# Where a burst schedule runs its transposed maxima and sums: behind a stretch of projection steps, or inside it

## The chip, the core and the metric

The kernel runs on one core of a Trainium2 chip. The metric is the device time of one execution in microseconds (us); less is better. The engines run side by side, each in its own program order, and wait for one another through semaphores: TensorE (PE; PEld is its loading of weights), VectorE (DVE), ScalarE (ACT), GpSimd (POOL) and SyncE (SP), which here only issues transfers (DMAs). SPq is SP's queue of them. Matmuls write into PSUM, whose banks are handed out by tags of a pool: a tile of a tag with three buffers can be written only when the reader of the tile three before it is done.

## What is computed

Two kinds of layer alternate, twice: windowed attention and a filter in the frequency domain. The input is 2048 tokens by 576 features, with 32 heads of 18 features.

```python
def _A_ref(x, wqkv, wo):
    H = 32; Dh = D // H; W = 256
    qkv = (x @ wqkv).reshape(B, S, 3, H, Dh).transpose(2, 0, 3, 1, 4)
    q, k, v = qkv[0], qkv[1], qkv[2]
    scores = jnp.einsum("bhqd,bhkd->bhqk", q, k) * (Dh ** -0.5)
    mask = (idx[:, None] - idx[None, :] >= 0) & (idx[:, None] - idx[None, :] < W)
    p = softmax(jnp.where(mask, scores, -1e9), axis=-1)
    o = jnp.einsum("bhqk,bhkd->bhqd", p, v)
    return o.transpose(0, 2, 1, 3).reshape(B, S, D) @ wo

def _B_ref(x, w_r, w_i):
    X = jnp.fft.rfft2(x, axes=(-2, -1)) * (w_r + 1j * w_i)
    return jnp.fft.irfft2(X, s=(S, D), axes=(-2, -1))

for layer in (_A_ref, _B_ref, _A_ref, _B_ref):
    x = x + layer(layernorm(x))
```

The change lies in the attention layer (`layer_a`), which runs twice.

## The kernel before

**Tiles.** The 32 heads go in eight groups (n) of four (two `pair` by two `hp`), the 2048 tokens in 16 tiles (i or j) of 128, and these in four columns (c) of 512. A number x stands for (n, i): x = 16 n + i, from 0 to 127.

**Projections.** Queries and keys come from `proj(i, c)`, which is 14 steps (L801), each one matmul of 512 columns into one PSUM tile `pj`. After the 14th, ACT copies the high part to `sg`, and DVE later subtracts it to get the low part (the "remainder", L816), which SP stores to DRAM with it (`qk_d<-sg`, L818). `stack_load(n, c)` brings rows of several heads back from there into `qs` and `ks`: twelve transfers on SP (L833).

**Scores and maxima.** `score_max(x, pair, hp)` makes one tile of scores on PE (S, L857), and DVE takes its row maxima under the mask into a column of `m` (L859: the reduction, and a reading of its accumulator). When the four tiles of a column c are done for all four heads, `m_rows(n, c)` brings the maxima into the queries: PE transposes `m` into a PSUM tile of tag S (`tpm`, L865), ACT negates it into `mt` (L867), and four transfers on SP put its rows into row 63 of `qs` (L872). From then on a product of `ks` and `qs` has the maximum already taken off.

**Exponentials, sums, norms.** `exps(x, pair, hp)` makes such a product (E, L889), ACT takes the exponential into `P` (L890), and POOL zeroes what the window leaves out (L892, L895). `part(x, half)` multiplies `P` with the values, which carry a column of ones so that the sums of the rows come with it, into the one PSUM tile U (L909). After four tiles ACT copies U into `us`, a single buffer (L914), and `norm(n, c)` finishes the column: four transpositions on PE into a tile of tag S (`tpo`, L923), the reciprocal of the sums (`rc`, L926) and the product (`o`, L928) on DVE, and a transfer to DRAM on SP (L933).

**The bursts.** Most of the layer's work runs in `bursts()` (L968 to L1011), 136 bursts numbered by k. Each takes three E (e) and three S (c), the latter ten x ahead (`LEAD`); on PE in the order S, E, E, E, S, S, so that DVE has the first of a burst's maxima before the others. Behind them come the remainders that are due, the parts of U that `gaps` gives to this burst, and, in every odd k, a stretch of projection steps: five, five and four in turn, so that three stretches are one projection of 14 steps (near the end: four, four, three, three). `loads(x)` calls `stack_load` at the start of the burst in which an x that is divisible by four begins, and its transfers enter SP's queue there. A group of maxima is complete, and is appended to the list `due`, in the burst whose scores reach the end of a column; a norm is appended after the part that fills U. Both come every 16 thirds of a burst. E needs a column's maxima two tiles ahead of its own, so that, between the last score of a column and the first E that uses its maxima, there are 16 E (in the first column of a head group there are 24). The list is worked off only behind a stretch:

```python
if k % 2:
    m = left.pop(0)
    for f in pj[at:at + m]:
        f()
    ends, at = at // 14 != (at + m) // 14, at + m
    for f, *a in due[:len(due) - 1 if ends else 2]:
        f(*a)
        due.pop(0)
```

`ends` is true where the stretch closes a projection; all but one of the list are then run, which with one item is none. Nothing is reordered by a scheduler: each engine runs its instructions in the order in which this program issues them.

Of the kernel before, what the change touches and what calls it, by code (L numbers as in the profile page):

```python
# [608 lines left out]
def layer_a(tc, ident, eps, bp, src, dst, wqk_d, wv_d, wo_d, dc_d, gc_d, dram, copy, wvs, second, spectral, share):  # L609
# [17 lines left out]
    if True:  # L627
# [134 lines left out]
        with ExitStack() as c2:  # L762
# [20 lines left out]
            def remainders():  # L783
                while ended:
                    ended.pop(0)()
# [60 lines left out]
            def score_max(x, pair, hp):  # L846

                n, i = divmod(x, NT)
                c, t = divmod(i, 4)
                q, k = qs[n % 2], ks_[n % 2]  # L850
                if (n, c) not in ms:
                    ms[n, c] = wp.tile([128, 2, 2, 4], F32, tag="m", name=f"m{n}_{c}", bufs=3)
                lo, hi = max(0, i - 2) * 128, (i + 1) * 128
                N = hi - lo
                b = 64 * hp
                ps = pp.tile([128, 512], F32, tag="S", name=f"S{x}_{pair}_{hp}", bufs=3)
                T.matmul(ps[:, 0:N], q[b:b + 63, pair, i * 128:i * 128 + 128], k[b:b + 63, pair, lo:hi], start=True, stop=True)  # L857
                jk = wp.tile([128, 384], BF, tag="jk", name=f"jk{x}_{pair}_{hp}", bufs=3)
                V.tensor_tensor_reduce(out=jk[:, 0:N], in0=ps[:, 0:N], in1=mask[:, 384 - N:384], scale=1.0, scalar=-3e38,  # L859
                                       op0=ALU.add, op1=ALU.max, accum_out=ms[n, c][:, hp, pair, t:t + 1])  # L860
# [16 lines left out]
            def exps(x, pair, hp):  # L877

                n, j = divmod(x, NT)
                q, k = qs[n % 2], ks_[n % 2]  # L880
                nq = min(3, NT - j) * 128
                hl_ = 2 * hp + pair
                if hp == pair == 0:
                    pt[n, j] = wp.tile([128, 4, 384], F32, tag="P", name=f"P{n}_{j}", bufs=6)
                p = pt[n, j]

                ps = pp.tile([128, 512], F32, name=f"E{x}_{hl_}", **(dict(tag="S", bufs=3) if pair and NX - LEAD <= x < NX - 4 else dict(tag="E", bufs=3)))
                b = 64 * hp
                T.matmul(ps[:, 0:nq], k[b:b + 64, pair, j * 128:j * 128 + 128], q[b:b + 64, pair, j * 128:j * 128 + nq], start=True, stop=True)  # L889
                A.activation(p[:, hl_, 0:nq], ps[:, 0:nq], AF.Exp, scale=SC)  # L890
                if hp == pair == 1:
                    P.affine_select(out=p[:, :, 0:128], in_=p[:, :, 0:128], pattern=[[0, 4], [1, 128]], compare_op=ALU.is_ge,  # L892
                                    fill=0.0, base=0, channel_multiplier=-1)
                    if nq == 384:
                        P.affine_select(out=p[:, :, 256:384], in_=p[:, :, 256:384], pattern=[[0, 4], [-1, 128]], compare_op=ALU.is_gt,  # L895
                                        fill=0.0, base=0, channel_multiplier=1)
# [3 lines left out]
            def part(x, half):  # L900
                n, i = divmod(x, NT)

                e = i - i % 2
                j = (i - 1, i - 2 + 2 * (i % 2))[half]
                q0 = e if j < i else i
                q1 = e + 2 if i - 1 == j else q0 + 1
                for h in range(4):
                    if j >= 0:
                        T.matmul(U[32 * h:32 * h + 19, (q0 % 4) * 128:(q0 % 4) * 128 + 128 * (q1 - q0)], vts[n][:, j, h],  # L909
                                 pt[n, j][:, h, (q0 - j) * 128:(q1 - j) * 128],  # L910
                                 start=j == max(e - 1, 0), stop=j == i or (i == e and j == i - 2), skip_group_check=True)
                if half and i % 4 == 3:
                    us[n, i // 4] = u = wp.tile([128, 512], F32, tag="us", name=f"us{n}_{i}", bufs=1)
                    A.copy(u, U)  # L914
# [32 lines left out]
            pj = [f for i in range(2, 9) for c in range(4) for f in proj(i, c, c % 2 if i == 2 else c == 0 and i == 3)]  # L947
            done, due = 0, []
# [4 lines left out]
            def loads(t):  # L953
                n, c = divmod(t + 20, NT)
                if c % 4 == 0 and 0 < n < NQ:
                    stack_load(n, c // 4)
                if t + LEAD == 5:
                    v_load(0)
                if t + 12 in range(NT, NX, NT):
                    v_load((t + 12) // NT)  # L960

            def copies(t):
                if copy and t >= 32 and t % 4 == 0 and t < 32 + 16 * len(copy):

                    z, r = divmod(t // 4 - 8, 4)
                    P.dma_start(*[a[32 * r:32 * r + 32] for a in copy[z]])

            def bursts():  # L968

                es = [(x, pair, hp) for x in range(2, MIX) for pair in range(2) for hp in range(2)]  # L970
                ss = [(x + LEAD, pair, 1 - hp) for x, pair, hp in es]
                left = [*(5, 5, 4) * 20, *(4, 4, 3, 3) * 2]
                gaps = {}
                for p in range(2 * MIX - 5):
                    g = 2 * ((p + 1) // 3)
                    if p % 8 == 0 and p and (p + 1) % 3:
                        g += (p + 1) % 3
                    elif p % 8 == 1 and p > 1 and (p + 1) % 3 == 2:
                        g += 1
                    gaps.setdefault(g, []).append(divmod(p, 2))  # L980
                at = done
                for k in range(len(es) // 3):
                    e, c = es[3 * k:3 * k + 3], ss[3 * k:3 * k + 3]
                    for x, pair, hp in e:
                        if pair == hp == 0:
                            loads(x)
                            copies(x)
                    score_max(*c[0])
                    for f in e:
                        exps(*f)  # L990
                    score_max(*c[2])
                    score_max(*c[1])
                    remainders()
                    for x, half in gaps.get(k, ()):
                        part(x, half)
                        if half and x % 4 == 3:
                            due.append((norm, *divmod(x // 4, 4)))
                    full = (3 * k + 3) // 4 + 11
                    if (3 * k) // 4 + 11 < full and full % 4 == 3:
                        due.append((m_rows, *divmod(full // 4, 4)))  # L1000
                    if k % 2:
                        m = left.pop(0)
                        for f in pj[at:at + m]:
                            f()
                        ends, at = at // 14 != (at + m) // 14, at + m
                        for f, *a in due[:len(due) - 1 if ends else 2]:
                            f(*a)
                            due.pop(0)
                remainders()
                part(MIX - 3, 1)  # L1010
                return at  # L1011
# [4 lines left out]
            for t in range(-LEAD, NX + 2):  # L1016
# [3 lines left out]
                if 2 <= t < MIX:  # L1020
                    if t == 2:
                        due.append((m_rows, 0, 2))
                        done = bursts()
                    continue
# [3 lines left out]
                ends = done // 14 != want // 14  # L1028
# [125 lines left out]
```

## Time and profile before

| | |
|---|---|
| median of three runs | 1581.59 us (1579.38 to 1583.68) |
| the profiled execution | 1575.97 us, its span 1574.2 us |
| mean granted TensorE clock | 0.978 |
| bursts of the first attention layer, first E to last | 145.27 to 452.16 us: 306.89 us |
| bursts of the second | 925.74 to 1236.07 us: 310.33 us |

A row of a group or of the order of time names the engine, the line, the operation and its tiles (written <- read), how many instructions it merges (x), and, in brackets or behind the last bar, how long the engine had stood idle before it and what ended that. A row of waits reads: who waited, for whom, us in total, how often, the longest. A row of a stage gives its bounds and length, the busy time of each engine with its number of instructions, the granted TensorE clock (1.00 is full speed), the share of the DMA engines and GB/s. In the order of time the first two numbers of a row are its start and its duration. Matmuls are pipelined: the step from start to start, not the duration, is what one costs.

### The profile page before, as it was taken

How to read it: one execution, taken by the hardware profiler on the slowest of the kernel's cores; microseconds unless marked ns; L12 is line 12 of the kernel's file. 1: busy time of each engine (PE TensorE's matmuls, PEld its weight loads, DVE VectorE, ACT ScalarE, POOL GpSimd, SP SyncE). 2: the span in 40 equal slices, each digit the busy share in tenths (PEclk: the TensorE clock that was granted, in tenths of full speed). 3: DMA queues.
4: the chain of work that ended last, by engine and by line, in shares of the span. 5: the costliest groups of instructions: out<-in, count | busy, mean ns of one | idle time of the engine just before them, and what ended most of it. 6: DMA issues, size and time to landing. Idle time of an engine off the chain costs nothing.

```text
span 1574.2 us, 34565 instructions
## 1 busy us (share of the span) xinstructions
PE 1486.6 (94%) x12124; PEld 1122.2 (71%) x12124; DVE 967.2 (61%) x3152; ACT 795.4 (51%) x1900; POOL 622.9 (40%) x1026
## 2 busy tenths in 40 slices
PE   7999999999899899999999999999989998999998
PEld 7975666565555899858999656665655558998598
DVE  4327777677675455456842467776776655554477
ACT  5524667566577244224454146665656673442243
POOL 2172345344356233153321823444333463322434
PEclk9999999999899999999999999999999999999999
DMA  6656555455354355767663674554543443657664
GB/s 191 187 177 210 157 166 178 154 176 159 118 155 129 119 184 182 233 234 233 236 163 89 195 213 138 163 152 121 152 141 110 139 134 117 202 186 244 208 217 137
DMA packets 203130, 267.63 MB, mean 170 GB/s; under 512 B 103182, under 2 KB 108302, under 8 KB 201998
## 3 DMA queue, kind: packets, MB, share of 16 engines
q1 hardware_dynamic: 194638, 245.44, 51.2%
q10 hardware_dynamic: 7680, 15.59, 2.9%
q0 software_dynamic: 640, 4.39, 0.9%
q8 instruction: 97, 1.59, 0.4%
q14 instruction: 75, 0.61, 0.1%
HBM read 166.71 MB, written 102.00 MB: 171 GB/s over the span
## 4 chain that ended last, share of the span: by engine, by line
PE 70%; DVE 8%; DMA 7%; ACT 4%; POOL 2%; issue 2%; SPq 1%; POOLq 0%; DVEq 0%; ACTq 0%
PE pj L801 15%; PE S L857 11%; PE U L909 10%; PE ops L555 6%; PE E L889 5%; PE vps L738 4%; PE pf L202 3%; PE pz L215 3%; PE tpo L923 2%; PE pi L361 2%; PE pq L313 2%; PE po L382 2%; PE p L294 2%; DMA ofree<-yd 1%; DMA qs<-mt 1%
## 5 line engine op out<-in xcount | busy, mean ns | idle before, releaser
L859 DVE CUSTOM_DVE_ANT_0 jk<-S,mask 128x384 bf16<-128x384 f32 (+2 forms) x1024 | 492.4, 528 | 159.5 <-PE E L889 83.7
L890 ACT ACTIVATE P<-E 128x384 f32<-128x384 f32 (+2 forms) x1024 | 411.3, 477 | 194.3 <-PE E L889 167.1
L892 POOL TENSOR_SCALAR_AFFINE_SELECT P<-P 128x512 f32<-128x512 f32 x256 | 162.3, 634 | 447.7 <-ACT P L890 422.5
L857 PE MATMUL S<-ks,qs 63*128 63x384 f32 (+2 forms) x1024 | 294.1, 385 | 8.0 <-DVE o L928 6.6
L889 PE MATMUL E<-qs,ks 64*128 64x384 f32 (+2 forms) x1024 | 233.1, 387 | 28.3 <-DMA qs<-mt 20.7
L857 PEld LDWEIGHTS S<-ks,qs 63*128 63x128 f32 x1024 | 151.6, 190 | 123.6 <-DVE m L859 66.0
L909 PE MATMUL U<-P,vq 128*19 128x128 f32 (+1 forms) x3840 | 200.0, 335 | 1.1 <-POOL P L895 0.5
L889 PEld LDWEIGHTS E<-qs,ks 64*128 64x128 f32 x1024 | 116.6, 190 | 59.3 <-issue 31.3
L801 PE MATMUL pj<-xh,wqh 128*128 128x512 f32 x360 | 151.8, 422 | 4.3 <-ACT vt L742 1.7
L909 PEld LDWEIGHTS U<-P,vq 128*19 128x19 f32 x3840 | 93.9, 99 | 80.1 <-issue 33.6
L895 POOL TENSOR_SCALAR_AFFINE_SELECT P<-P 128x512 f32<-128x512 f32 x224 | 142.0, 634 | 0.0
L555 PE MATMUL ops<-oroom 128*128 128x288 f32 x840 | 123.5, 303 | 4.4 <-DVE oroom L538 3.0
L801 PE MATMUL pj<-xh,wql 128*128 128x512 f32 x360 | 125.4, 422 | 0.1
L801 PE MATMUL pj<-xl,wqh 128*128 128x512 f32 x288 | 120.6, 419 | 0.0
L555 PEld LDWEIGHTS ops<-oroom 128*128 128x128 f32 x840 | 115.5, 193 | 6.2 <-DVE oroom L538 4.0
L801 PEld LDWEIGHTS pj<-xh,wqh 128*128 128x128 f32 x360 | 68.8, 191 | 31.1 <-issue 6.3
L171 POOL TENSOR_TENSOR eo<-xn 128x287 f32<-128x287 f32 x32 | 26.1, 816 | 155.0 <-ACT xn L169 143.9
L813 ACT CAST sg<-pj 128x512 fp32r<-128x512 f32 x72 | 42.2, 587 | 89.2 <-PE pj L801 87.8
L859 DVE DVE_READ_ACCUMULATOR2_ANT m<- 128x1 f32 x1024 | 84.6, 83 | 0.0
L801 PEld LDWEIGHTS pj<-xh,wql 128*128 128x128 f32 x360 | 64.3, 191 | 25.2 <-issue 13.7
L361 PE MATMUL pi<-oroom 128*128 128x256 f32 (+1 forms) x576 | 76.4, 286 | 4.5 <-ACT oroom L346 3.2
L816 DVE TENSOR_TENSOR sg<-pj,sg 128x512 fp32r<-128x512 f32 x72 | 49.4, 687 | 45.5 <-ACT sg L813 45.5
(177 smaller groups left out, 2602.3 us busy)
## 6 DMA issues: line engine op xcount, KB each, us to landing
qk_d<-sg SPq DMA_DIRECT2D x56, 512.0 KB
qs<-qk_d SPq DMA_DIRECT2D x384, 72.0 KB
ks<-qk_d SPq DMA_DIRECT2D x384, 72.0 KB
v_d<-vt SPq DMA_DIRECT2D x32, 304.0 KB
vq<-v_d SPq DMA_DIRECT2D x16, 608.0 KB
yd<-ye SPq DMA_DIRECT2D x32, 290.0 KB
wt<-in_w SPq DMA_DIRECT2D x16, 580.0 KB
x<-ofree SPq DMA_DIRECT2D x32, 288.0 KB
```

The lines of the kernel that those rows point to most:

```text
L361: T.matmul(o, z[:, sl, c, lo:lo + m], mo, start=k == 0, stop=k == 5)
L555: self.nc.tensor.matmul(self.ps[u][n][:, 0:288], x, self.w[p][:, wk * D + n * 288:wk * D + n * 288 + 288], start=first and i == 0, stop=la ...
L738: T.matmul(ps[:, n, 0:288], xT(xk, c), w[:, wk, n * 288:(n + 1) * 288], start=i == 0, stop=i == len(ks) - 1)
L801: T.matmul(box["ps"].rearrange("r (n p) -> r n p", n=NT) if second else box["ps"], w[:, wk], x, start=s == 0, stop=s == len(ks) - 1)
L816: V.tensor_sub(rest[:, 1], by, rest[:, 0].bitcast(F32))
L857: T.matmul(ps[:, 0:N], q[b:b + 63, pair, i * 128:i * 128 + 128], k[b:b + 63, pair, lo:hi], start=True, stop=True)
L859: V.tensor_tensor_reduce(out=jk[:, 0:N], in0=ps[:, 0:N], in1=mask[:, 384 - N:384], scale=1.0, scalar=-3e38, op0=ALU.add, op1=ALU.max, accu ...
L889: T.matmul(ps[:, 0:nq], k[b:b + 64, pair, j * 128:j * 128 + 128], q[b:b + 64, pair, j * 128:j * 128 + nq], start=True, stop=True)
L890: A.activation(p[:, hl_, 0:nq], ps[:, 0:nq], AF.Exp, scale=SC)
L892: P.affine_select(out=p[:, :, 0:128], in_=p[:, :, 0:128], pattern=[[0, 4], [1, 128]], compare_op=ALU.is_ge, fill=0.0, base=0, channel_mult ...
L895: P.affine_select(out=p[:, :, 256:384], in_=p[:, :, 256:384], pattern=[[0, 4], [-1, 128]], compare_op=ALU.is_gt, fill=0.0, base=0, channel ...
L909: T.matmul(U[32 * h:32 * h + 19, (q0 % 4) * 128:(q0 % 4) * 128 + 128 * (q1 - q0)], vts[n][:, j, h], pt[n, j][:, h, (q0 - j) * 128:(q1 - j) ...
```

## The change

In every odd burst, the list `due` is sorted so that maxima (`m_rows`) come before sums (`norm`); one item of it, or two if it holds more than two, is run between the second and the third step of the stretch, whether or not the stretch ends a projection. Nothing is run behind the stretch any more. No instruction of the computation is added or taken away.

```diff
                     if k % 2:
                         m = left.pop(0)
-                        for f in pj[at:at + m]:
+                        due.sort(key=lambda z: z[0] is norm)
+                        for s, f in enumerate(pj[at:at + m]):
+                            if s == 2:
+                                for g, *a in due[:1 + (len(due) > 2)]:
+                                    g(*a)
+                                    due.pop(0)
                             f()
-                        ends, at = at // 14 != (at + m) // 14, at + m
-                        for f, *a in due[:len(due) - 1 if ends else 2]:
-                            f(*a)
-                            due.pop(0)
+                        at += m
```

Worked out by hand from these lines, the list never holds more than two when it is run, so that each stretch runs one item at most. In each layer 26 groups of maxima and 25 norms pass through it.

## The prediction

> **What bounds the kernel now.** I read the page first, then the waits of TensorE (PE) inside the two stretches in which bursts run (147 to 452 us and 930 to 1236 us), then the order of time around one wait, then a table of stages.
>
> ```profile
> PE 1486.6 (94%) x12124; PEld 1122.2 (71%) x12124; DVE 967.2 (61%) x3152; ACT 795.4 (51%) x1900; POOL 622.9 (40%) x1026
> ...
> L889 PE MATMUL E<-qs,ks 64*128 64x384 f32 (+2 forms) x1024 | 233.1, 387 | 28.3 <-DMA qs<-mt 20.7
> ```
>
> PE is the bound, with VectorE (DVE) far behind it, so a microsecond in which PE stands still in a burst is lost, and one on another engine is lost only if PE waits for it. The last row names the one large wait: the products for the exponentials (E) wait for the row of maxima, which goes from `mt` into `qs` by DMA. Inside the bursts:
>
> ```profile
> PE E L889 <- DMA qs<-mt: 8.5, 2, 5.9
> PE S L857 <- DVE o L928: 3.3, 14, 0.3
> PE E L889 <- DMA qs<-mt: 8.9, 3, 6.2
> PE S L857 <- DVE o L928: 3.3, 14, 0.3
> ```
>
> The first two rows are layer one, the others layer two: 17.4 us in 5 waits for maxima; the rest of the 20.7 lies ahead of the bursts, where nothing changes. One of them in order of time, TensorE and then the DMA queue of SyncE (SPq):
>
> ```profile
> 282.11 0.50 PE L801 MATMUL pj<-xl,wqh 128*128 128x512 f32 x1
> 282.45 0.39 PE L801 MATMUL pj<-xh,wqh 128*128 128x512 f32 x1
> 282.68 0.40 PE L801 MATMUL pj<-xl,wqh 128*128 128x512 f32 x1
> 282.91 0.63 PE L801 MATMUL pj<-xh,wql 128*128 128x512 f32 x2
> 283.44 0.28 PE L865 MATMUL tpm<-ident,m 128*16 128x128 f32 x1
> 283.65 0.43 PE L857 MATMUL S<-ks,qs 63*128 63x384 f32 x1
> 286.74 1.13 PE L889 MATMUL E<-qs,ks 64*128 64x384 f32 x3 [2.65 <-DMA qs<-mt]
> ...
> 277.81 2.45 SPq L833 DMA_DIRECT2D qs<-qk_d  x6
> 280.30 3.17 SPq L833 DMA_DIRECT2D ks<-qk_d  x6
> 283.74 4.96 SPq L872 DMA_DIRECT2D qs<-mt  x8
> ```
>
> This is burst 63 (k in `bursts`) of layer one, and E at 286.74 opens burst 64. The maxima it needs had been transposed in burst 61; but the twelve loads of that same burst stand ahead of them on SP and hold it from 277.81 to 283.47, so their four transfers go out only at 283.74, together with the four of the next group. By the code this meeting of loads and maxima happens in bursts 13, 61 and 109 of each layer. Burst 13 transposes a group whose user is two x later than usual, and nothing waits there; 61 and 109 give two stalls a layer.
>
> **What a stall costs.** The stages below run from the first E of burst 15 to that of 19, of 63 to 67, and of 111 to 115, in both layers; the parts repeat every 48 bursts, so that the work is the same and the first of each layer is undisturbed. The last row is the time right behind the stall above.
>
> ```profile
> core 0: us, PE busy (x) PEld busy (x) DVE busy (x) ACT busy (x) POOL busy (x), PEclk, DMA share, GB/s
> 176.95:185.41 8.46, 8.42 (x87) 5.00 (x84) 5.88 (x23) 4.88 (x15) 3.21 (x6) 1.00 0.30 80
> 281.39:294.18 12.79, 10.13 (x71) 6.02 (x68) 6.25 (x25) 6.44 (x15) 4.16 (x8) 0.73 0.36 113
> 389.87:406.79 16.92, 11.03 (x87) 6.52 (x83) 4.93 (x25) 6.32 (x15) 4.10 (x8) 0.70 0.47 145
> 958.25:966.72 8.47, 8.43 (x87) 4.99 (x83) 5.87 (x23) 4.88 (x15) 3.21 (x6) 1.00 0.30 86
> 1063.46:1077.21 13.75, 10.97 (x71) 5.96 (x68) 6.78 (x25) 6.37 (x15) 4.38 (x8) 0.77 0.35 106
> 1173.83:1189.92 16.09, 9.94 (x88) 5.76 (x84) 4.88 (x25) 6.24 (x15) 3.52 (x7) 0.79 0.51 129
> 286.80:292.60 5.80, 5.80 (x27) 3.61 (x29) 2.65 (x10) 3.63 (x8) 1.69 (x3) 0.50 0.27 83
> ```
>
> The disturbed stages are longer by 12.79 - 8.46 = 4.33, 16.92 - 8.46 = 8.46, 13.75 - 8.47 = 5.28 and 16.09 - 8.47 = 7.62 us: 25.7 us. Of that 17.4 is standing still; the other 8.3 is PE running at half its clock afterwards (0.50 in the last row).
>
> **The change, part by part.** *Maxima two bursts earlier.* The old code emptied the list after a stretch of projections, and held one item back in a stretch that ends a projection; the new one takes one item in every stretch, a maximum first. So the groups transposed in 13, 61 and 109 move to 11, 59 and 107, and their four SP transfers move ahead of the twelve loads (and of a store of `sg`, which does not wait for them long: `mt` is one ACT operation behind the burst's exponentials). Loads of 12 issues, 5.66 us from the rows, now stand between transposition and use only where they did no harm before. No other group of maxima falls into a burst with loads. I take the whole 25.7; bounds: nothing, if the rows land late all the same, and 25.7.
>
> *Transposing after two steps.* What is queued behind a waiting transposition on PE is the rest of the stretch and then the next burst's scores, for which DVE waits. There are 26 groups a layer in bursts. A group whose last score is the first of its burst, or lies in the burst before, finds its maxima ready; so does the PSUM bank, that of the burst's first score. But where 3k + 3 is a multiple of 16 (k = 15, 31, 47, 63, 79, 95, 111, 127) the last of the burst's three scores belongs to the group:
>
> ```profile
> 282.35 0.08 DVE L859 DVE_READ_ACCUMULATOR2_ANT m<- 128x1 f32 x1
> 282.82 0.08 DVE L859 DVE_READ_ACCUMULATOR2_ANT m<- 128x1 f32 x1
> 283.30 0.08 DVE L859 DVE_READ_ACCUMULATOR2_ANT m<- 128x1 f32 x1
> ```
>
> The first maximum is there at 282.43, ahead of 282.68, when the third step now begins and the transposition would; the last is there at 283.38. In the old place the transposition starts at 283.44; in the new one it starts at 283.44 too, and three steps of 0.23 (282.45 to 282.68) then follow: 0.69 us. In 47, 95 and 127 no transposition stood before, and the wait is 283.44 - 282.68 = 0.76. Two layers of 5 x 0.69 + 3 x 0.76: 11.5 us lost. DVE, which has nothing to do meanwhile, cannot give it back. Bounds: 0, if DVE is ahead by then, and 52 x 0.76 = 39.5, if all wait for the last maximum; I take 11.5, since each of the three readings above ends by itself and a wait can name it.
>
> *Sums after two steps.* Here the norm's four transpositions (`tpo`) came last, and DVE's reciprocal and product held the bank that the next burst's last score wants:
>
> ```profile
> 274.52 0.26 DVE L926 RECIPROCAL rc<-tpo 128x16 f32<-128x16 f32 x1 [0.60 <-PE tpo L923]
> 274.82 0.46 DVE L928 TENSOR_TENSOR o<-tpo,rc 128x288 f32<-128x288 f32 x1
> ...
> 275.42 0.41 PE L857 MATMUL S<-ks,qs 63*128 63x384 f32 x1 [0.28 <-DVE o L928]
> ```
>
> DVE itself stood idle for 0.60 us before them, until the transposition came. In the new place its 0.26 + 0.46 us fall in with the two or three steps left (0.46 to 0.69 us) and with the first score and three E of the next burst, which come ahead of the score in question; the 28 waits of this kind, 3.3 us a layer, go: 6.6 us gained (bounds 0 and 6.6; I take it all, since the work fits into that time). Most norms move one stretch later; the next copy of U into the single buffer `us` is 5.33 bursts after the last, so that nothing waits for it, and their `o` stores, now partly behind loads on SP, are read long after the bursts.
>
> *Cutting the run of steps.* A score that follows a step directly, and a step that follows a transposition (of the other layer stage, the nearest there is):
>
> ```profile
> 183.21 0.40 PE L801 MATMUL pj<-xh,wql 128*128 128x512 f32 x1
> 183.53 0.44 PE L857 MATMUL S<-ks,qs 63*128 63x384 f32 x1
> ...
> 65.01 0.27 PE L472 MATMUL tpba<-ident,atl 128*128 128x128 f32 x1
> 65.03 0.51 PE L738 MATMUL vps<-wvh,xh 128*128 128x288 f32 x2
> ```
>
> From the second step of five to the next score PE needed 3 x 0.23 to the fifth, 0.23 to the transposition and 0.21 to the score (282.45, 282.68, 283.44, 283.65), 1.13 us. Now it is 0.23 to the transposition, 0.02 to the third step, 0.34 to the fourth (what the first step of a run takes, 282.11 to 282.45), 0.23, and 0.32 to the score: 1.14. I take nothing. If instead each cut costs that first step's surplus, 0.11 us, the 51 of each layer come to 11 us, and if each saves as much, to -11; the range keeps them.
>
> **The sum.** -25.7 + 11.5 - 6.6 = -20.8 us. The profiled execution took 1575.97 us (its span and what lies around it), so its like would take 1555.2. The median of the runs is 1581.59, 5.6 above it; carried over: 1560.8, which I round to 1561.
>
> **Rivals.** *The new waits cool the clock* (slower). Sixteen gaps of up to 0.76 us arise beside the steps, and a short gap can be enough:
>
> ```profile
> 476.90:480.30 3.40, 2.92 (x17) 1.58 (x17) 2.91 (x13) 3.38 (x10) 2.96 (x5) 1.00 0.02 5
> 480.40:483.70 3.30, 3.30 (x24) 1.63 (x25) 1.57 (x7) 1.84 (x5) 2.26 (x3) 0.50 0.01 3
> ```
>
> Behind the bursts, 3.40 us with only 0.48 idle are followed by 3.30 at half clock, a loss of up to 1.65 us. Sixteen of these are 26.4: 1561 + 26 = 1587. It decides from 13 on (20.8 / 1.65). Against it: the stretch there has no projections, and the 28 waits of 0.3 at most in the bursts left the clock alone. Chance 0.09.
>
> *The rows land late all the same.* Then 11.5 - 6.6 = +4.9: 1586.5. For it: eight issues took 4.96 us on a crowded queue; against it, the four of burst 59 no longer stand behind 5.66 us of loads, and go out two bursts earlier. Chance 0.08.
>
> *Only the standing still comes back*: half clock turns up elsewhere, as it does behind 480.4. Gain 17.4 in place of 25.7: 1569. Chance 0.12. The Trainium skill ("TensorE: Matmul & The Clock Gate", Part 1: The HAM clock gate) has the clock fall only after at least one whole idle window of about 3.4 us; by that rule the slow 5.80 us here are not the work of a gap of 2.65 us, and would stay. The row with 0.50 right behind a 2.65 us gap speaks against the rule.
>
> *The three steps hide the wait* and DVE is ready: -32.3, 1549. The three readings speak against it. Chance 0.05.
>
> **How the numbers follow.** The forecast has 0.66. This kernel's measurement can tell some 0.3% (4.7 us) from nothing. Faster: 0.66 + 0.12 + 0.05 = 0.83; slower 0.14, since one of the rivals on that side lies near the border, and 0.03 between. The range of 1552 to 1575 holds the forecast with most of either bound on cutting, the third rival, and most of the fourth; the two slower cases (0.17) stay outside.
>
> **What would show it.** Waits for `qs<-mt` inside the bursts gone, and stages 63 to 67 and 111 to 115 near 9.2 us at clock 1.00 (8.46 and one wait); `tpm` in burst 63 0.7 us after the second step, with three steps behind it, and a wait of at most 0.76 us before it in eight bursts a layer alone; S no longer waiting for `o`. Waits before all 26, or 0.50 behind them, would make the forecast wrong, and so would a wait of E that stays.

## The result

| | median, us | range, us | runs |
|---|---|---|---|
| before | 1580.49 | 1576.1 to 1583.68 | 4 |
| after | 1542.47 | 1538.92 to 1545.29 | 4 |

The ratio is 0.976, 95% interval 0.9728 to 0.9792: faster by 38.0 us, where 20.8 had been forecast (1561), and outside the range on the fast side. The profiled executions differ by less, 30.7 us, because the one of before (1575.97) is among the quickest of its runs and the one of after (1545.29) is the slowest of its own.

The page of after, in the rows that answer to those of before:

```profile
PE 1471.5 (95%) x12124; PEld 1106.1 (72%) x12124; DVE 968.7 (63%) x3152; ACT 789.7 (51%) x1900; POOL 623.0 (40%) x1026
...
L889 PE MATMUL E<-qs,ks 64*128 64x384 f32 (+2 forms) x1024 | 234.6, 386 | 11.0 <-ACT P L890 8.8
```

The idle time before E falls from 28.3 to 11.0 us, and `qs<-mt` no longer ends most of it. TensorE is still the bound. Its waits inside the bursts, the first two rows from 147 to 431 us (layer one), the last from 915 to 1201 us (layer two):

```profile
PE tpm L865 <- DVE m L859: 4.2, 7, 0.6
PE tpm L865 <- DMA ks<-qk_d: 0.6, 1, 0.6
PE tpm L865 <- DVE m L859: 4.7, 8, 0.6
```

Both kinds of wait of before are gone, E for the maxima and S for `o`. In their place are sixteen waits of the transposition, 9.5 us in all, 0.60 each (one of them is put down to a load, but stands in the same place). Burst 63 of layer one in order of time, TensorE and then the DMA queue of SyncE around it, each row a start and a duration:

```profile
278.33 0.51 PE L801 MATMUL pj<-xl,wqh 128*128 128x512 f32 x1
278.68 0.39 PE L801 MATMUL pj<-xh,wqh 128*128 128x512 f32 x1
279.66 0.28 PE L865 MATMUL tpm<-ident,m 128*16 128x128 f32 x1 [0.60 <-DVE m L859]
279.70 0.47 PE L801 MATMUL pj<-xl,wqh 128*128 128x512 f32 x1
280.01 0.63 PE L801 MATMUL pj<-xh,wql 128*128 128x512 f32 x2
```

```profile
270.99 2.44 SPq L872 DMA_DIRECT2D qs<-mt  x4
...
274.18 2.50 SPq L833 DMA_DIRECT2D qs<-qk_d  x6
...
280.27 2.46 SPq L872 DMA_DIRECT2D qs<-mt  x4
```

The transposition starts 0.98 us after the second step, 0.75 later than the next step would have, and three steps follow it. The four rows of the earlier group now go out at 270.99, ahead of the loads at 274.18, and the four of burst 63 are alone at 280.27; before, eight went out together at 283.74.

Stages of after: the bursts of each layer from the first E of burst 3 to the first E behind burst 135 (burst 1 is left out, since the clock at its start differs from run to run), then bursts 63 to 67 and 111 to 115 of both layers, then a stretch behind the bursts. Columns as before: bounds, length, busy time by engine, granted clock, DMA share, GB/s.

```profile
151.39:431.33 279.94, 274.60 (x2728) 168.80 (x2724) 219.32 (x869) 188.52 (x476) 129.70 (x208) 1.00 0.56 168
919.42:1201.59 282.17, 276.02 (x2727) 168.85 (x2724) 219.42 (x869) 188.63 (x476) 122.04 (x192) 1.00 0.54 151
...
277.61:286.64 9.03, 8.43 (x74) 4.98 (x70) 6.86 (x29) 6.16 (x15) 4.25 (x8) 1.00 0.44 111
379.02:388.76 9.74, 9.13 (x92) 5.35 (x88) 5.80 (x29) 6.16 (x15) 4.18 (x8) 1.00 0.68 188
1046.81:1055.86 9.05, 8.46 (x74) 4.99 (x71) 6.86 (x29) 6.16 (x15) 3.78 (x7) 1.00 0.42 115
1149.02:1158.79 9.77, 9.18 (x90) 5.36 (x86) 5.78 (x29) 6.16 (x15) 3.71 (x7) 1.00 0.79 169
...
448.50:472.40 23.90, 23.61 (x149) 12.44 (x151) 14.82 (x56) 13.10 (x35) 12.32 (x16) 0.50 0.04 9
```

The same two stages of before:

```profile
151.48:451.18 299.70, 286.42 (x2727) 179.26 (x2724) 218.34 (x869) 191.40 (x476) 129.93 (x210) 0.97 0.52 158
932.53:1234.71 302.18, 287.65 (x2726) 178.63 (x2722) 218.38 (x871) 191.15 (x476) 122.33 (x194) 0.98 0.49 141
```

So the bursts take 279.94 + 282.17 = 562.1 us instead of 601.9, a gain of 39.8, at full clock throughout. The forecast of 20.8 was one for this stretch. Behind the bursts these two executions differ the other way, by 6.8 us; a section below looks at that.

### The profile page after: what moved, and what is told of

It reads as the page before. It is cut to its first block, busy times and chain, and to the rows that moved or that the text cites. A ratio compares the mean times of both kernels' runs of the same rounds, so it can differ in the third digit from the quotient of the medians.

```text
span 1543.6 us, 34591 instructions
## 1 busy us (share of the span) xinstructions
PE 1471.5 (95%) x12124; PEld 1106.1 (72%) x12124; DVE 968.7 (63%) x3152; ACT 789.7 (51%) x1900; POOL 623.0 (40%) x1026
## 4 chain that ended last, share of the span: by engine, by line
PE 69%; DVE 8%; DMA 7%; ACT 4%; POOL 3%; issue 2%; SPq 1%; POOLq 0%; DVEq 0%; ACTq 0%
PE pj L801 15%; PE S L857 10%; PE U L909 10%; PE ops L555 6%; PE E L889 6%; PE vps L738 4%; PE pf L202 3%; PE pz L215 3%; PE tpo L923 2%; PE pi L361 2%; PE po L382 2%; DMA ofree<-yd 2%; DVE jk L859 2%; PE pq L313 1%; PE p L294 1%
## 5 line engine op out<-in xcount | busy, mean ns | idle before, releaser
L857 PE MATMUL S<-ks,qs 63*128 63x384 f32 (+2 forms) x1024 | 277.8, 382 | 0.5 <-DVE m L859 0.3
L857 PEld LDWEIGHTS S<-ks,qs 63*128 63x128 f32 x1024 | 145.2, 189 | 113.1 <-DVE m L859 67.7
L801 PE MATMUL pj<-xh,wqh 128*128 128x512 f32 x360 | 156.7, 435 | 3.5 <-ACT vt L742 1.7
L801 PE MATMUL pj<-xh,wql 128*128 128x512 f32 x360 | 124.4, 417 | 0.1
L171 POOL TENSOR_TENSOR eo<-xn 128x287 f32<-128x287 f32 x32 | 26.1, 816 | 157.3 <-ACT xn L169 146.2
L801 PEld LDWEIGHTS pj<-xh,wql 128*128 128x128 f32 x360 | 63.5, 189 | 21.3 <-issue 12.9
L361 PEld LDWEIGHTS pi<-oroom 128*128 128x128 f32 (+1 forms) x576 | 72.9, 186 | 7.0 <-ACT oroom L346 4.8
```

Source lines behind the costliest of these rows:

```text
L361: T.matmul(o, z[:, sl, c, lo:lo + m], mo, start=k == 0, stop=k == 5)
L801: T.matmul(box["ps"].rearrange("r (n p) -> r n p", n=NT) if second else box["ps"], w[:, wk], x, start=s == 0, stop=s == len(ks) - 1)
```

## Experiments

The theory in most of them: the gain comes in part from the order of the list (maxima two bursts earlier, no stall) and in part from the place of the norms (after two steps instead of behind the last). The rivals: the order alone does it, or the maxima's place helps too. Every edit but two is made to the changed kernel. "Bursts" is always the sum over both layers from the first E of burst 3 to the first E behind burst 135, in the profiled execution.

| kernel | median, us | ratio to before, 95% | bursts, us |
|---|---|---|---|
| before | 1580.49 | | 601.9 |
| after | 1542.47 | 0.976, 0.9728 to 0.9792 | 562.1 |
| all behind the stretch | 1562.68 | 0.992, 0.9893 to 0.9946 | 583.9 |
| norms behind | 1566.54 | 0.9925, 0.9901 to 0.9949 | 587.6 |
| maxima behind | 1536.72 | 0.9759, 0.9722 to 0.9796 | 558.4 |
| old order, norms cut in | 1563.84 | 0.9918, 0.9887 to 0.9949 | 581.4 |
| old order, two loads later | 1561.08 | 0.9849, 0.9766 to 0.9931 | 574.7 |
| two groups of maxima late | 1563.63 | 0.9876, 0.9825 to 0.9927 | 583.5 |
| norms ahead of the last step | 1562.45 | 0.9861, 0.9807 to 0.9915 | 576.4 |
| split one step later | 1533.4 | 0.9669, 0.9606 to 0.9733 | 561.9 |
| sixteen maxima behind | 1535.91 | 0.9702, 0.9634 to 0.977 | 553.4 |
| split two steps later, sixteen maxima behind | 1522.77 | 0.9612, 0.9561 to 0.9662 | 553.0 |
| `o` twice, norms behind | 1592.82 | 1.0063, 1.003 to 1.0097 | 611.2 |
| `o` twice, as after | 1560.89 | 0.9855, 0.9804 to 0.9907 | 582.9 |

Each ratio is to runs of before on the same chip, whose medians go from 1577.83 to 1585.2, so that it says more than the difference of two medians of the table; the interval of the kernel with later loads is wide, its four runs lie between 1545.94 and 1568.77.

### Order and places, two by two

The list of the changed kernel, in its new order, with norms and maxima each either after two steps or behind the stretch:

```diff
-for s, f in enumerate(pj[at:at + m]):
-    if s == 2:
-        for g, *a in due[:1 + (len(due) > 2)]:
-            g(*a)
-            due.pop(0)
-    f()
+now = [due.pop(0) for _ in range(min(len(due), 1 + (len(due) > 2)))]
+for s, f in enumerate([*pj[at:at + m], None]):
+    for g, *a in now:
+        if s == PLACE:
+            g(*a)
+    if f:
+        f()
```

`PLACE` is `m` for all behind, `(m if g is norm else 2)` for norms behind, and `(2 if g is norm else m)` for maxima behind.

> The new order of the list and one item in every stretch, but everything run behind the stretch. Theory (a wait costs what lies from start to start, so a norm behind a stretch costs some 0.46 us and not the 0.24 of idle shown; the surplus of the change came from the norms): the four stalls for qs<-mt go, 25.7 us, the 16 waits before tpm go, and the norms' waits stay: 1580 - 26 = 1554 (1551 to 1558). Rival (the surplus came from the order itself, from one item a stretch): 1580 - 37 + (no waits before tpm) -11 = 1532 to 1543.

> As the changed kernel, but norms run behind the stretch and only maxima cut it. Theory: -25.7 + 11.5 = -14 against before: 1566 (1562 to 1570). Rival (the surplus of 16 us came from maxima in the middle of the stretch, norms are worth 6.6): -38 + 6.6: 1549.

> As the changed kernel, but maxima run behind the stretch and only norms cut it. Theory: the 16 waits of tpm for DVE, 11.5 us, go, and all gains stay: 1542 - 11.5 = 1531 (1527 to 1535). Rival (the surplus came from maxima in the middle): 1580 - 25.7 - 6.6 = 1548.

The bursts in stages, all behind:

```profile
151.07:441.94 290.87, 284.45 (x2726) 178.62 (x2722) 218.29 (x869) 190.24 (x476) 130.39 (x210) 1.00 0.55 162
922.02:1215.08 293.06, 286.26 (x2727) 178.89 (x2724) 218.32 (x868) 190.25 (x476) 122.41 (x193) 1.00 0.52 147
```

Maxima behind:

```profile
149.59:427.83 278.24, 277.14 (x2726) 173.98 (x2722) 219.71 (x869) 189.19 (x476) 130.36 (x210) 1.00 0.57 170
913.43:1193.59 280.16, 278.37 (x2726) 174.07 (x2722) 219.83 (x871) 189.16 (x476) 122.80 (x194) 1.00 0.54 153
```

With after's two rows and the 587.6 us of norms behind, the four new-order kernels give the two effects twice each. Cutting the norms in: 583.9 to 558.4 with the maxima behind, 587.6 to 562.1 with them cut in, -25.5 both times, 0.51 for each of the 50 norms. Cutting the maxima in: 583.9 to 587.6 and 558.4 to 562.1, +3.7. The effects simply add. The order alone: 601.9 to 583.9, -18.0. Together -18.0 - 25.5 + 3.7 = -39.8, which is all of it. Of the expectations, that for all behind lay some 9 us too low and that for maxima behind some 6; the sections below say where the rest lies. The rival by which the order alone does it falls; so, over all maxima together, does the one by which their place helps.

### The stalls by themselves

The kernel before, unchanged but for the loads of bursts 61 and 109, which are issued behind the list's work instead of at the start of the burst, with the copies that stand beside them (in layer one GpSimd has one in each of these bursts, in layer two none):

```diff
-for x, pair, hp in e:
-    if pair == hp == 0:
-        loads(x)
-        copies(x)
+late = [x for x, pair, hp in e if pair == hp == 0]
+for x in late if k not in (61, 109) else ():
+    loads(x)
+    copies(x)
...
+if k in (61, 109):
+    for x in late:
+        loads(x)
+        copies(x)
```

> As the kernel before, but in bursts 61 and 109 the twelve loads are issued behind the maxima and not ahead of them; nothing moves on TensorE, VectorE or ScalarE. Theory (SP's order makes the stalls): the four waits of E for qs<-mt go, 25.7 us: 1580 - 26 = 1554 (1551 to 1558). Rival (the rows land late because they are transposed late): no change, 1580.

SyncE's queue in that kernel, the burst of layer one in which loads and maxima meet:

```profile
279.35 2.46 SPq L872 DMA_DIRECT2D qs<-mt  x4
281.91 2.23 SPq L833 DMA_DIRECT2D qs<-qk_d  x6
```

With the maxima's rows ahead of the loads, no wait for `qs<-mt` is left in the bursts, and they take 574.7 us: -27.2, 13.5 of it in layer one and 13.7 in layer two, where nothing but the loads moved. That is the price of the stalls, 25.7 in the prediction. The old order can thus be saved in this way too.

The reverse, on the changed kernel: the groups of bursts 59 and 107 are held back to 61 and 109, behind the loads, still after two steps.

```diff
-if s == 2:
-    for g, *a in due[:1 + (len(due) > 2)]:
+if s == 2 and k not in (59, 107):
+    for g, *a in due[:2 if k in (61, 109) else 1 + (len(due) > 2)]:
```

> As the changed kernel, but the maxima of bursts 59 and 107 wait for bursts 61 and 109, where they run before the norm, after two steps, and behind the loads on SP. Theory: the four stalls come back, with the slow clock behind them: 1542 + 26 = 1568 (1560 to 1572). Rival (they were late for another reason, or a maximum after two steps is early enough): 1542 to 1546.

Waits of E in its bursts, layer one and layer two:

```profile
PE E L889 <- DMA qs<-mt: 5.7, 2, 4.1
PE E L889 <- DMA qs<-mt: 5.8, 2, 4.0
```

The waits are back, in two places a layer, and the bursts take 583.5 us, 21.4 more than after. They are shorter than before's 8.5 and 8.9, since the transposition stands three steps earlier in its burst; 21.4 falls short of the price of the stalls as well, probably for the same reason.

### The norms: price and dose

The kernel before with its own order, the norms alone cut in after two steps and the maxima behind:

```diff
-for f in pj[at:at + m]:
-    f()
-ends, at = at // 14 != (at + m) // 14, at + m
-for f, *a in due[:len(due) - 1 if ends else 2]:
-    f(*a)
-    due.pop(0)
+ends = at // 14 != (at + m) // 14
+now = [due.pop(0) for _ in range(min(len(due), max(len(due) - 1, 0) if ends else 2))]
+for s, f in enumerate([*pj[at:at + m], None]):
+    for g, *a in now:
+        if s == (2 if g is norm else m):
+            g(*a)
+    if f:
+        f()
+at += m
```

> As the kernel before, with its list, its bursts for every item and its maxima behind the stretch; only norms run between the second and the third step. Theory: stalls for qs<-mt stay as they were, the norms' waits go: 1580 - 23 = 1557 (1553 to 1561). Rival (what the profile shows as idle is all): 1580 - 6.6 = 1573.

The bursts take 581.4 us, -20.5 with the stalls still there. A norm's place alone is worth as much as the whole forecast. Of it 24.3 us are gained in the bursts with norms and those behind them, and 3.8 lost in others, which was not followed. The median of 1563.84 is above the 1557 expected: the bursts gained less than the 23 of the theory, and in the profiled execution 7.2 us are lost behind them (124.4 against 117.2, the stretch of the last section).

Then the dose. On the changed kernel, norms one step from the end, `PLACE` being `(m - 1 if g is norm else 2)`; and twice the product `o`, by issuing L928 a second time with the same operands, which gives the same values and one more DVE operation of 0.46 us in each norm, once with the norms behind and once as after.

> As the changed kernel, but norms run one step before the end of the stretch and not after the second. Theory: one step of 0.23 us covers VectorE's work only in part, so that of some 0.46 us a norm 0.23 remains, 50 times: 1542 + 11 = 1553 (1549 to 1557). Rival (any step behind the norm is enough, or the saving lies in another thing than the wait for o): 1542.

> As norm_behind (norms behind the stretch, maxima after two steps), but VectorE computes each o twice, the same values into the same tile. Theory (a norm behind a stretch costs because VectorE holds the bank for the next burst's last score): each of 50 norms costs 0.46 us more: 1566 + 23 = 1589 (1583 to 1595). Rival (the cost of its place lies on TensorE, in the switch between kinds of matmuls): 1566.

> As the changed kernel (norms after two steps), but VectorE computes each o twice. Theory: the steps behind the norm cover 0.46 us more only in part, in stretches of five more than in stretches of four: 1542 + 5 to 18. Rival (VectorE is idle a third of the time and covers all of it): 1542.

Bursts 13 and 14 of layer one together, with a norm in a stretch of five steps: 5.08 us with the norm behind, 4.84 with one step left, 4.45 with three (after). With the double product: 5.57 behind, 4.87 in the new place. Over all norms, one step left costs 14.3 us more than after, 0.29 a norm, and the median was 9 us above the number expected. The second product costs 23.7 us behind, 0.47 each, its full duration; and still 20.8 in the new place, 0.42 each, a little more than expected. So DVE's time between the transposition and the release of the bank is what TensorE pays for, and the two or three steps behind the new place cover one product but have no room for another.

Where the price hides can be read from burst 13 with all behind, TensorE and DVE:

```profile
174.11 0.60 PE L923 MATMUL tpo<-ident,us 128*128 128x128 f32 x4
...
175.10 0.34 PE L857 MATMUL S<-ks,qs 63*128 63x384 f32 x1
175.64 0.41 PE L857 MATMUL S<-ks,qs 63*128 63x384 f32 x1 [0.20 <-DVE o L928]
...
175.04 0.46 DVE L928 TENSOR_TENSOR o<-tpo,rc 128x288 f32<-128x288 f32 x1
```

And after:

```profile
172.35 0.60 PE L923 MATMUL tpo<-ident,us 128*128 128x128 f32 x4
...
174.02 0.34 PE L857 MATMUL S<-ks,qs 63*128 63x384 f32 x2
```

Behind, the last score starts 0.54 us after the one before it, and the row shows 0.20 idle: the idle time counts only from the modelled end of the earlier score, at 175.44. After, both start so closely together that one row merges them. Taken from start to start, the 28 waits of before come to 0.53 to 0.66 us each, 16.1 in all, where their rows show 6.6.

Nor are these all. Burst 21 of before holds a norm and, behind it in the same stretch, a group of maxima; TensorE, then VectorE:

```profile
192.76 0.27 PE L865 MATMUL tpm<-ident,m 128*16 128x128 f32 x1
...
193.42 0.84 PE L857 MATMUL S<-ks,qs 63*128 63x384 f32 x2
...
193.25 0.46 DVE L928 TENSOR_TENSOR o<-tpo,rc 128x288 f32<-128x288 f32 x1
```

The merged row holds two scores that start 0.44 us apart, with no idle time that would name a wait. But the second starts 0.148 us after `o` ends (193.859, 193.711). So it is with every norm of before: in all 50 the last score of the next burst starts 0.147 or 0.148 us after the end of `o`. In 28 the profile shows idle time before it; in the other 22, with maxima behind the norm, it shows next to none, and from start to start these cost 0.43 to 0.47 us each, 10.0 in all. Together that is 26.1 us, where 6.6 is shown. With the norms cut in after two steps, these steps of the same norms come to 2.9 us in the old order, and in the changed kernel to 2.7 for the 48 with a burst behind them.

Why did the order alone gain 18.0, when the stalls were worth 27.2? The other 9.2 are lost. The waits in the bursts of layer one with all behind seem to show where:

```profile
PE S L857 <- DVE o L928: 5.3, 24, 0.3
```

In the old order 14 norms a layer show such a wait; sorted, with one item to a stretch, it is 24. But the ten more had cost their time before without a row: from start to start these scores come to 26.1 us in the old order and 26.8 with all behind, so that the norms explain some 0.7. By pairs of bursts, against the kernel with later loads, 4.2 us lie in six places a layer where the sorted list runs the maxima in a stretch that ends a projection and the norm in the next, instead of the other way round; what that costs a group of maxima behind the stretch, the next section shows. Another 6.5 lie in the fourteen places a layer where a stretch that held both is split in two (bursts 21 to 24 took 4.42 + 3.66 = 8.08 us before and take 3.59 + 4.98 = 8.57 apart, one of the largest such differences); some 1.4 are gained elsewhere. The cause of these two stays open.

### The sixteen waiting maxima

Where 3k + 3 is a multiple of 16 the maxima go behind the stretch, all else as after: `PLACE` is `(2 if g is norm or (3*k+3) % 16 else m)`.

> As the changed kernel, but the eight maxima of each layer whose last score is the last of its burst's three (3k + 3 a multiple of 16) run behind the stretch; the other maxima and all norms still cut it. Theory: the sixteen waits before tpm go, some 8.5 us by the pairs of bursts that hold them, and what the other cuts gave stays: 1542 - 9 = 1533 (1529 to 1537). Rival (what a maximum waits for in the stretch is given back in the next burst): 1542.

The bursts take 553.4 us, 8.7 less than after, 8.2 of it in the bursts of the sixteen. So the waits do cost; but the other 34 maxima are better off after two steps. Why, burst 59 shows, with the maxima behind:

```profile
268.80 0.27 PE L865 MATMUL tpm<-ident,m 128*16 128x128 f32 x1
269.00 0.59 ACT L813 CAST sg<-pj 128x512 fp32r<-128x512 f32 x1 [0.58 <-PE pj L801]
...
269.34 0.90 PE L857 MATMUL S<-ks,qs 63*128 63x384 f32 x2
269.48 0.26 ACT L867 ACTIVATE mt<-tpm 16x128 fp32r<-16x128 f32 x1
```

And after:

```profile
270.39 0.28 PE L865 MATMUL tpm<-ident,m 128*16 128x128 f32 x1
270.70 0.27 ACT L867 ACTIVATE mt<-tpm 16x128 fp32r<-16x128 f32 x1 [0.24 <-PE tpm L865]
271.17 0.59 ACT L813 CAST sg<-pj 128x512 fp32r<-128x512 f32 x1 [0.20 <-PE pj L801]
271.34 0.39 PE L857 MATMUL S<-ks,qs 63*128 63x384 f32 x1
271.41 0.39 PE L857 MATMUL S<-ks,qs 63*128 63x384 f32 x1
```

Behind a stretch that ends a projection, ACT's cast of 0.59 us stands ahead of `mt` and holds up the release of the bank: the two later scores, merged in one row, stretch over 0.90 us. After two steps `mt` is done before the cast begins. Between the kernel with maxima behind and the one after, the burst pairs of the sixteen grow by 8.5 us and those of the other 34 shrink by 6.9 (5.2 of it in the twelve that end a projection); those with norms grow by 2.0, whose cause was not sought. That is 3.6, the +3.7 up to rounding.

### What is given back behind the bursts

A stretch with equal work behind the bursts, from the first E there to the same E in the output stage; before, in both layers:

```profile
451.18:508.28 57.10, 52.86 (x558) 29.14 (x554) 34.90 (x128) 43.38 (x110) 35.84 (x56) 0.97 0.43 131
1234.71:1294.81 60.10, 55.06 (x558) 29.74 (x554) 35.08 (x128) 43.52 (x110) 35.82 (x56) 0.91 0.41 123
```

After:

```profile
431.33:495.83 64.50, 59.60 (x558) 32.22 (x554) 35.56 (x129) 43.81 (x110) 35.43 (x56) 0.81 0.38 112
1201.59:1261.09 59.50, 54.07 (x558) 29.41 (x554) 35.18 (x129) 43.39 (x110) 35.36 (x56) 0.94 0.41 122
```

124.0 us against 117.2, at a lower clock in layer one: 7.4 lost there, 0.6 won in layer two. Over the span 39.8 - 6.8 = 33.0 would be left, and 30.6 is (1574.2 to 1543.6); the last 2.4 were not followed. What stands there, in the order of time of TensorE and of ACT:

```profile
448.24 0.52 PE L889 MATMUL E<-qs,ks 64*128 64x384 f32 x1 [2.05 <-ACT P L890]
...
447.13 0.67 ACT L506 CAST oroom<-ofree 128x576 fp32r<-128x576 f32 x1 [2.45 <-DMA ofree<-in_wo]
```

ACT's first cast of the output weights waits 2.45 us for their load; the exponentials stand behind it on ACT, and E behind them. TensorE is idle for 2.05 us and then runs 23.9 us at half clock (the stage 448.50 to 472.40 above). The wait is not new. Before, in layer one:

```profile
465.29 0.67 ACT L506 CAST oroom<-ofree 128x576 fp32r<-128x576 f32 x1 [0.87 <-DMA ofree<-in_wo]
```

In layer two it was 1.70 us before and 2.10 after. The load goes out at 460.29 and 440.68 us, 9.11 and 9.35 us behind the bursts, and the cast starts 5.00 us behind that before and 6.45 after: the load took longer. Why, was not sought. How long the cast waits differs from kernel to kernel and from layer to layer, but over the traces of all fourteen kernels, two layers each, it divides them: in the five places where it waits 0.87 us or less, the stretch takes 55.1 to 57.1 us at a granted clock of 0.97 to 1.00; in the other 23, where it waits 1.28 to 4.62, it takes 59.5 to 66.0 at 0.77 to 0.94. The cast comes one step later in the first of the next two kernels, two steps and with the sixteen maxima behind in the second:

```diff
-if 0 <= t - (OB - 12) < 10 and (t - (OB - 12)) % 2 == 0:
-    out.split((t - (OB - 12)) // 2)
+if 0 <= t - (OB - 11) < 10 and (t - (OB - 11)) % 2 == 0:
+    out.split((t - (OB - 11)) // 2)
```

> As the changed kernel, but ScalarE's splits of the output weights behind the bursts stand one x later. Theory: in the profile of the changed kernel the first split waited for the load of these weights, E stood still for 2.05 and 1.71 us behind it and the clock then went to half; without it 3 to 8 us less: 1535 to 1539. Rival (the time until the next thing that ends late is set elsewhere): 1542.

> As max_mixed, and ScalarE's splits of the output weights behind the bursts stand two x later. Theory: both savings add: 1533 less 3 to 9: 1527 (1521 to 1532). Rival (the later splits push something behind them): 1533 or more.

One step later alone gives a median of 1533.4, its runs from 1525.6 to 1540.81. In the profiled execution, the slowest of these, layer one is rid of the wait (56.4 us), layer two still waits 1.42 (61.3). Two steps (`OB - 10`), with the maxima mixed, in the same stretch behind the bursts:

```profile
427.18:482.28 55.10, 51.27 (x558) 28.23 (x555) 35.20 (x129) 43.06 (x110) 35.38 (x56) 1.00 0.45 132
1181.05:1236.15 55.10, 51.28 (x560) 28.29 (x556) 35.22 (x130) 43.05 (x110) 35.37 (x56) 1.00 0.44 133
```

No wait of the cast, full clock, and 55.1 us in both layers. This kernel beats both: 1522.77 us, 0.9612 of before (0.9561 to 0.9662).

## Why the prediction was wrong

**Maxima two bursts earlier: right.** -25.7 was forecast from the stages; moving the loads alone gave -27.2. With the stalls their half clock went too, as the stages 63 to 67 and 111 to 115 say: 9.03, 9.74, 9.05 and 9.77 us at clock 1.00, two near the 9.2 foretold and two some 0.5 above it, the sum down from 59.55 to 37.59. The rivals with late rows and with only the standing still coming back fall. By the rule of the Trainium skill quoted there ("TensorE: Matmul & The Clock Gate", Part 1: The HAM clock gate), a gap shorter than a whole window would not have lowered the clock, and the half clock would have stayed; these stages, and the 23.9 us at 0.50 behind a gap of 2.05 us, differ from it.

***Sums after two steps*: the step that failed.** The mechanism held: VectorE's work on the late transposition keeps the bank from the next burst's last score, and the two or three steps behind the new place cover it. The price did not, in both of its factors. The step counted the 28 scores before which the profile shows idle time, but all 50 norms made one wait; and it took 6.6 us from that idle time, also as its upper bound, but a late matmul costs what it adds from start to start, 26.1 us for the 50. That the idle time ended where a modelled duration ended was known; the Trainium skill has it too ("Perfetto Trace Analysis", Tensor Engine Instruction: the end of a matmul is an estimate). For the wait quoted there, the score ahead of it gives the price, 0.66 us from start to start beside the 0.28:

```profile
274.76 0.39 PE L857 MATMUL S<-ks,qs 63*128 63x384 f32 x1
275.42 0.41 PE L857 MATMUL S<-ks,qs 63*128 63x384 f32 x1 [0.28 <-DVE o L928]
```

Measured: -25.5 for the norms' new place, where -6.6 was forecast.

***Transposing after two steps*: right for the maxima that wait.** The sixteen waits stand in the eight bursts a layer that were named, 0.60 idle each. Against the kernel with later loads, which is the old order without the stalls, these sixteen bursts, each with the burst behind it, grew by 11.5 us in all, as forecast. The transposition of burst 63 came 0.98 us after the second step, with three steps behind it. What the step put at nothing, the other 34, is not nothing: sorted, twelve of them come into stretches that end a projection, which goes with a loss of 4.2 us as long as they stand behind the stretch, and cutting the 34 in gives 6.9 back, most of it by ACT's `mt` going ahead of the cast.

**Cutting the run of steps: not separated.** The four new-order kernels leave no room for more than a small sum: the 22 maxima that neither wait nor end a projection gain 0.08 us each when cut in. (The 1.13 us that the prediction reads for the uncut run is 1.20 by its own rows, from 282.45 to 283.65.)

**The sum.** By terms the misses are -27.2 + 25.7 = -1.5 for the maxima, nothing for the sixteen waits, and -25.5 + 6.6 = -18.9 for the sums. The order and the maxima's place cost 9.2 + 3.7 = 12.9, of which 11.5 lie at the sixteen; the 1.4 left is in no term of the prediction. Together that is -19.0, the difference of -39.8 and -20.8. The stretch behind the bursts takes back 6.8 in the profiled execution, which the prediction did not see; the medians, 38.0 apart, suggest that it was less in others.

**Rivals.** The new waits did not cool the clock: PEclk is 1.00 over both burst stages. The rival in which the three steps hide the wait came nearest in time (1549), but by luck: the waits are there.

## What to carry to other kernels

Price a wait on a pipelined engine from start to start against the same instruction without the wait, and count the waits by what their start follows, not by the rows that show idle time; the idle column showed 28 of 50 waits here, and 6.6 us of 26.1. Here a tile of a shared PSUM tag was written at the end of a dense run, and its reader's time fell on the next user of the tag: put the write as many steps ahead as the reader needs, but not ahead of data that isn't ready, as sixteen maxima and fifty sums of the same list show. After a gain, look at the next thing timed by a transfer: here a cast that waited 0.87 and 1.70 us for its weights before waited 2.45 and 2.10 after, and with its place two steps on the stretch behind the bursts took 9.4 us less in layer one and 4.4 less in layer two.

## Not expected of the hardware

The clock does not follow the length of a gap alone. Sixteen gaps of 0.60 us beside dense projection steps left it at 1.00 over 562 us of bursts; before, a gap of 2.65 us was followed by 5.80 us at 0.50; and behind the bursts a shorter one, 2.05 us, was followed by 23.9 us at 0.50, in a stretch that keeps TensorE less dense (at full clock it is busy for 51.27 of 55.10 us there in the last kernel, and for 274.60 of 279.94 in the bursts after). What in that stretch keeps the clock down was not tried by itself.
